# The last 192 columns of a step of experts 0 to 3 take rounded tokens and residuals side by side in one matmul

## The chip, the cores and the metric

The kernel runs on one core of a Trainium2 chip. The metric is the device time of one launch in microseconds: the median of three runs was 637.49 (637.31 to 637.5). A core has a matrix engine (TensorE, PE in the profile, with its weight loads as PEld), VectorE (DVE), ScalarE (ACT), GpSimd (POOL) and SyncE (SP). All run their own instruction streams in order and wait for one another through semaphores. Matmuls read from SBUF and sum into banks of PSUM, which hold 512 float32 values per partition; ACT and DVE take the sums out of there.

## The reference

For 2048 tokens of width 448 the kernel gives `g * a + (1 - g) * b`. Here `a` is the real part of a two-dimensional Fourier transform by dense matrices, `g` a sigmoid of a weighted sum of the token, and `b` a mixture of 8 experts with the two best per token:

```
gates = softmax(xt @ wg);  topk_idx = argsort(-gates)[:, :2];  topk_g normalised to 1
h = gelu(einsum("nd,edf->nef", xt, w1))     # d = 448, f = 1792, tanh form of gelu
y = einsum("nef,efd->ned", h, w2)
b = einsum("ne,ned->nd", cw, y)             # cw: topk_g of the chosen experts, else 0
```

All inputs are float32, and so is the output.

## The kernel before, in words

The transform and the routing come first, up to some 38 us. Then the experts run in the order of their load, each over the tokens that chose it, gathered into columns: `CAPS = (576, 544, 544, 544, 512, 512, 512, 496)` columns for experts 0 to 7. An expert has 14 steps (`NF`), one for each 128 of the 1792 hidden features, so there are 112 jobs `u = (e, f)`.

Both products are made of rounded numbers. A float32 operand is split into a part rounded to the engine's fast type (fp32r) and the residual, rounded too; a product is then hi x hi plus hi x lo plus lo x hi. The tokens of expert `e` stand as `XH[e]` (rounded, 4 chunks of 128 features, the last chunk with its residual in the upper 64 partitions) and `XL[e]` (residuals of the first 3 chunks), written by `turn` (L649 to L660) or, for expert 0, `turn0` and `left0` (L662 to L679). The weights of a job are `hi` and `lo` for the first product, `up` and `dn` for the second, rounded by ACT in `upper` (L205) and by DVE in `lower` (L210).

`up(u)` (L731 to L765) makes the first product and the gelu. Experts 0 to 3 have more than 512 columns and take two halves of `cap // 2`, expert 0 in its first step 256 and 320; experts 4 to 7 take one. Each half is 11 matmuls into one of three `acc` banks: 3 of `hi` with `XH`, 3 of `hi` with `XL`, 1 of `hi` with the last chunk, 4 of `lo` with `XH` (L744 to L747). Before each, its 128x128 weights are loaded. ACT takes the gelu from PSUM into `g` (L748). DVE then casts `g` to `gh` (L756) and subtracts to get `gl` (L757); the columns above 512 are kept apart (L762, or L764 for expert 0).

`down(u)` (L767 to L795) makes the second product: for each of 4 tiles of 128 tokens three matmuls of 448 columns, `gh` with `up`, `gh` with `dn`, `gl` with `up` (L786 to L790), summed over the 14 steps in the banks `Y`. The 32 tokens above 512 of experts 1 to 3 go through `few` (L796 to L811) twice an expert. At an expert's end `combine` (L828) scales the sums, two tiles on DVE and two on ACT, and POOL scatters them into the output.

The order on PE, DVE, ACT and SP is written out by hand. In the main loop (L1034 to L1053) an iteration issues: `turn` of the next expert's tokens if due, rounding of the weights of job `u + 2`, `blocks` (a DVE transpose of gathered tokens, L646) and the gathers on POOL if due, then `up(u + 1)`, `down(u)`, and `side_work`. The last does the checks of the transform's matrices on DVE (two a step for most of experts 1 to 6, L874), the blending of the transform's outputs and their sending. So on DVE the order is weights' residuals, transpose, `gh`, `gl`, rest, checks. On PE a job's second product stands one iteration behind its first.

Of the kernel before, what the change touches and what calls it, by code (L numbers as in the profile page):

```python
# [10 lines left out]
F32R = mybir.dt.float32r  # L11
# [3 lines left out]
AF = mybir.ActivationFunctionType  # L15
OP = mybir.AluOpType
AX = mybir.AxisListType

P = 128
# [4 lines left out]
NC = 4  # L24
# [4 lines left out]
CMAX = max(CAPS)  # L29
# [10 lines left out]
Q = 32  # L40
# [14 lines left out]
LOTS = (0, 6, NF)  # L55
BANKS = (0, 1, 2, 4, 3)
AHEAD = 5
FAR = 65536.0
HERE = 8192.0
SLACK = 2.0 ** -36  # L60
# [2 lines left out]
def r32(ap):  # L63
    return ap.bitcast(F32)


def tiles_of(cap):
    return [min(P, cap - c * P) for c in range((cap + P - 1) // P)]
# [3 lines left out]
def tile_kernel(ctx: ExitStack, tc: tile.TileContext, xt, xrows, xplain, wg, whid, cq, cw, cspec, edge, refs, wquad, whall, cgen, wcat, out):  # L72
    nc = tc.nc
    te, ve, se, gp, sp = nc.tensor, nc.vector, nc.scalar, nc.gpsimd, nc.sync
# [110 lines left out]
    def fetch(k, hold=False):  # L185
        if k >= len(jobs):
            return
        e, f = jobs[k]
        RAW[k] = [stream.tile([P, NC * P], F32, name="raw"), stream.tile([P, D], F32, name="row", bufs=NF - LOTS[1] + AHEAD)]
        if hold:  # L190
# [7 lines left out]
    def apart(e):  # L198
        return CAPS[e] - FULL * P == Q
# [25 lines left out]
    def be(ap):  # L225
        return ap[:, None, :].to_broadcast([P, NT, E])
# [12 lines left out]
    def routing():  # L239
# [89 lines left out]
        ve.tensor_scalar(top, st0, -HERE, None, op0=OP.add)  # L329
        ve.scalar_tensor_tensor(spot, past, FAR, pos, op0=OP.mult, op1=OP.add)  # L330
        ve.tensor_tensor(spot, spot, be(top), OP.add)
# [93 lines left out]
        ve.tensor_tensor(dl, dl, st0, OP.subtract)  # L425
        ve.tensor_scalar(dl, dl, -FAR, None, op0=OP.add)
        ve.tensor_tensor(past, past, be(dl), OP.mult)
# [92 lines left out]


    tl0 = tiles_of(CAPS[0])
    XH, XL = {}, {}

    XG, XQ = {}, {}

# [101 lines left out]
    xp = ctx.enter_context(tc.tile_pool(name="xp", bufs=2))  # L628
# [19 lines left out]

    def turn(e, c):  # L649
        if c == 0:  # L650
            XH[e] = xp.tile([P, NC, CMAX], F32R, name="XH")
            XL[e] = xp.tile([P, NC - 1, CMAX], F32R, name="XL")
        k, xq = XQ.pop((e, c))
        src = xq[:, :k].rearrange("p q c t -> p c q t")
        sl = slice(c * P, c * P + k * Q)
        h = XH[e][:, :, sl].rearrange("p c (q t) -> p c q t", t=Q)
        l = XL[e][:, :, sl].rearrange("p c (q t) -> p c q t", t=Q)
        se.activation(h, src, AF.Copy)
        ve.tensor_tensor(l, src[:, : NC - 1], r32(h[:, : NC - 1]), OP.subtract)
        ve.tensor_tensor(h[64:P, NC - 1], src[64:P, NC - 1], r32(h[64:P, NC - 1]), OP.subtract)  # L660

    def turn0(c, n):  # L662
        if c == 0:
            XH[0] = xp.tile([P, NC, CMAX], F32R, name="XH")
            XL[0] = xp.tile([P, NC - 1, CMAX], F32R, name="XL")
        pt = (psy if c > 1 else ps).tile([P, NC, P], F32, name=f"y{c - 2}" if c > 1 else "acc")
        xg = XG.pop(c)
        for k in range(NC):
            te.transpose(pt[:, k, :n], xg[:n, k * P : (k + 1) * P], ident[:n, :n])  # L669
        sl = slice(c * P, c * P + n)  # L670
        se.activation(XH[0][:, :, sl], pt[:, :, :n], AF.Copy)
        TU[c] = pt, sl, n

    TU = {}

    def left0(c):
        pt, sl, n = TU.pop(c)
        ve.tensor_tensor(XL[0][:, :, sl], pt[:, : NC - 1, :n], r32(XH[0][:, : NC - 1, sl]), OP.subtract)  # L678
        ve.tensor_tensor(XH[0][64:P, NC - 1, sl], pt[64:P, NC - 1, :n], r32(XH[0][64:P, NC - 1, sl]), OP.subtract)  # L679

    def due(e, step, pace):
        c = step // pace
# [2 lines left out]
    def turn_due(e, step, lag, pace):  # L685
        c = due(e, step - lag - 1, pace)
        if c is not None:
            turn(e, c)
# [15 lines left out]
    for m in range(NQT):  # L704
        odd(m, 6)
    turn0(0, tl0[0])
    odd(0, 7)
    left0(0)
    odd(1, 7)
    turn0(1, tl0[1])  # L710
    odd(2, 7)
    left0(1)
    odd(3, 7)
    turn0(2, tl0[2])
    left0(2)
    turn0(3, tl0[3])
    middle()
# [13 lines left out]
    def up(u):  # L731
        e, f = jobs[u]
        hi, lo = W[u]
        cap = CAPS[e]
        rem = max(0, cap - FULL * P)
        g = mp.tile([P, CMAX], F32, name="g")
        nh = 1 if cap <= 512 else 2
        cut = 2 * P if u == 0 else cap // nh
        for hf in range(nh):
            cs = slice(hf * cut, cap if hf == nh - 1 else cut)  # L740
            n = cs.stop - cs.start
            acc = ps.tile([P, 512], F32, name="acc")
            part = lambda w, x, c: (w[:, c * P : (c + 1) * P], x[e][:, c, cs])
            steps = [part(hi, XH, c) for c in range(NC - 1)] + [part(hi, XL, c) for c in range(NC - 1)]  # L744
            steps += [part(hi, XH, NC - 1)] + [part(lo, XH, c) for c in range(NC)]
            for s, (a, b) in enumerate(steps):
                te.matmul(acc[:, :n], a, b, start=s == 0, stop=s == len(steps) - 1)  # L747
            se.activation(g[:, cs], acc[:, :n], AF.Gelu_apprx_tanh)  # L748
        if u == last:
            gh, gl = (stream.tile([P, DX], F32R, name=n) for n in ("hi", "lo"))  # L750
        else:
            gh = mp.tile([P, CMAX + RMAX], F32R, name="gh", bufs=3)
            gl = mp.tile([P, FULL * P], F32R, name="gl", bufs=3)
        main = cap - rem
        top = main if apart(e) else cap
        ve.tensor_copy(gh[:, :top], g[:, :top])  # L756
        ve.tensor_tensor(gl[:, :main], g[:, :main], r32(gh[:, :main]), OP.subtract)  # L757
        if apart(e):
            if f in LOTS:
                rt["rest"] = mp.tile([P, NF - LOTS[1], Q], F32, name="rest", bufs=2)  # L760
            REST[u] = rt["rest"][:, f - max(b for b in LOTS if b <= f)]
            ve.tensor_copy(REST[u], g[:, main:cap])  # L762
        elif rem:
            ve.tensor_tensor(gh[:, cap : cap + rem], g[:, main:cap], r32(gh[:, main:cap]), OP.subtract)  # L764
        GH[u] = (gh, gl)  # L765
# [265 lines left out]

    advance(2)
    up(UP)
    for u in range(UP, last):  # L1034
        e, f = jobs[u]
        plan = (e + 1, f - 1, 2, 2) if e else (1, f - 6, 2, 1)
        turn_due(*plan)
        prep(u + 2)
        if u < UP + SIDE:
            advance(2)  # L1040
            clear(2 * (u - UP))
            clear(2 * (u - UP) + 1)
        if u == last - NF - 1:
            tc.keep_in_program_order(gp.drain())
        if u == UP + SIDE:
            for _ in route:
                pass
            ck = late.enter_context(tc.tile_pool(name="ck", bufs=2, side="right"))
        stage(*plan)
        up(u + 1)  # L1050
        if u < last - 3:
            down(u)
        side_work(u - UP)  # L1053
# [11 lines left out]
    with tc.For_i(0, n_ov) as j:  # L1065
# [25 lines left out]
        pt = ps.tile([P, NC, P], F32, name="acc")  # L1091
# [5 lines left out]
        for f in range(NF):  # L1097
            raw = [stream.tile([P, NC * P], F32, name="raw"), stream.tile([P, D], F32, name="row", bufs=NF - LOTS[1] + AHEAD)]
            for t, b in zip(raw, SIDES):
                sp.dma_start(t, wcat[bass.ds(ej, 1), f, :, b].rearrange("o p n -> (o p) n"))  # L1100
            acc = ps.tile([P, 512], F32, name="acc")
# [18 lines left out]
    with tc.For_i(0, n_a) as j:  # L1120
# [3 lines left out]
        for h in range(2):  # L1124
            hf = full.tile([P, 2 * D], F32, name="hf")
            for u in range(2):
                acc = ps.tile([P, 512], F32, name="acc")
# [4 lines left out]
    with tc.For_i(0, n_b) as i:  # L1132
        acc = psy.tile([P, 512], F32, name="y0")
# [125 lines left out]
```

## Time and profile before

| | us |
|---|---|
| median of three runs | 637.49 |
| the profiled execution | 637.86 |
| its span, first to last instruction | 635.9 |
| PE busy | 625.9 (98%) |
| DVE busy | 506.9 (80%) |
| ACT busy | 248.5 (39%) |
| POOL busy | 205.1 (32%) |

Busy time counts each engine's own instructions in the span of the profiled execution. Matmuls overlap in their pipeline, so a matmul's duration is longer than what it costs; the distance from one start to the next is what it takes of PE's time. A row of the timeline merges neighbours of one kind: the start of the first, the time to the end of the last, and their count behind an x. Behind a row stands the idle time before it in brackets and what ended it.

### The profile page before, as it was taken

Reading aid. Unit: us, or ns where it says so; the run is one execution under the profiler, and the core shown is the slowest. Engines: PE = TensorE matmul, PEld = TensorE weight load, DVE = VectorE, ACT = ScalarE, POOL = GpSimd, SP = SyncE. Lnnn points to the kernel's source line nnn. Section 1 sums busy time; section 2 is a strip of 40 time slices with the busy share of each in tenths; the row PEclk is TensorE's granted clock in tenths of the full one; section 3 lists DMA queues with packets and bytes.
Section 4 is the critical chain, followed back from the end, with each engine's and each line's share of the span. In section 5 each row is a group of like instructions: output and inputs, shape, how many; then the busy total and the mean of one; then the engine's idle time right before and its main releaser. Section 6 shows DMA issues by size and latency. Waiting matters only on the chain.

```text
span 635.9 us, 11090 instructions
## 1 busy us (share of the span) xinstructions
PE 625.9 (98%) x3721; PEld 563.8 (89%) x3721; DVE 506.9 (80%) x1258; ACT 248.5 (39%) x504; POOL 205.1 (32%) x194
## 2 busy tenths in 40 slices
PE   9999999999999999999999999999999999999994
PEld 5999999998998989989899788888888888888884
DVE  7889797689987899779898799988997788555560
ACT  2553233343344434353343534433343434534440
POOL 1210074554144141443340443432331442141123
PEclk9999999999999999999999999999999999999998
DMA  8546454795766865596566767779456737766755
GB/s 346 183 149 210 155 184 140 245 238 192 237 207 160 257 226 197 197 262 196 176 243 234 229 170 244 266 234 276 136 183 195 152 115 150 166 136 145 156 74 65
DMA packets 52319, 122.78 MB, mean 193 GB/s; under 512 B 7488, under 2 KB 32208, under 8 KB 50208
## 3 DMA queue, kind: packets, MB, share of 16 engines
q1 hardware_dynamic: 40944, 101.94, 47.2%
q0 software_dynamic: 11168, 20.00, 18.2%
q8 instruction: 31, 0.51, 0.3%
q14 instruction: 32, 0.26, 0.1%
q10 hardware_dynamic: 144, 0.07, 0.0%
HBM read 105.89 MB, written 16.08 MB: 192 GB/s over the span
## 4 chain that ended last, share of the span: by engine, by line
PE 94%; issue 3%; POOL 1%; DVE 1%; POOLq 0%; ACT 0%; DVEq 0%; ACTq 0%
PE acc L747 45%; PE y L790 42%; PE y L807 1%; PE acc L512 1%; PE y L555 1%; POOL out L843 1%; PE y L474 1%; PE y L116 1%; PE acc L453 0%; POOL out L995 0%; PE acc L404 0%; PE y L669 0%; PE acc L669 0%; POOLq L1028 0%; PE acc L373 0%
## 5 line engine op out<-in xcount | busy, mean ns | idle before, releaser
L748 ACT ACTIVATE g<-acc 128x272 f32<-128x272 f32 (+4 forms) x168 | 78.0, 467 | 318.2 <-issue 178.9
L637 POOL DMA_INDIRECT xg<-xrows,piece x115 | 120.5, 1048 | 226.2 <-DVE xq L646 154.3
L790 PE MATMUL y<-up,gh 128*128 128x448 f32 (+1 forms) x458 | 167.7, 366 | 0.1
L790 PE MATMUL y<-dn,gh 128*128 128x448 f32 (+1 forms) x458 | 167.6, 366 | 0.0
L747 PE MATMUL acc<-XH,hi 128*128 128x272 f32 (+4 forms) x672 | 163.8, 325 | 0.0
L790 PE MATMUL y<-up,gl 128*128 128x448 f32 (+1 forms) x444 | 162.7, 366 | 0.0
L747 PE MATMUL acc<-XH,lo 128*128 128x272 f32 (+4 forms) x672 | 134.9, 322 | 0.0
L747 PEld LDWEIGHTS acc<-XH,hi 128*128 128x128 f32 x672 | 115.2, 188 | 11.2 <-ACT hi L205 1.8
L747 PEld LDWEIGHTS acc<-XH,lo 128*128 128x128 f32 x672 | 105.9, 188 | 8.4
L756 DVE CAST gh<-g 128x512 fp32r<-128x512 f32 (+2 forms) x111 | 48.1, 433 | 81.0 <-ACT g L748 80.6
L747 PE MATMUL acc<-XL,hi 128*128 128x272 f32 (+4 forms) x504 | 107.8, 322 | 0.0
L843 POOL DMA_INDIRECT out<-ys,tok x36 | 61.9, 1721 | 112.5 <-ACT ys L839 71.2
L790 PEld LDWEIGHTS y<-up,gh 128*128 128x128 f32 (+1 forms) x458 | 85.8, 187 | 8.1 <-issue 0.3
L790 PEld LDWEIGHTS y<-dn,gh 128*128 128x128 f32 (+1 forms) x458 | 85.8, 187 | 7.8
L874 DVE CUSTOM_DVE_ANT_0 junk<-quads 128x512 f32<-128x512 f32 x128 | 88.1, 688 | 2.2
L790 PEld LDWEIGHTS y<-up,gl 128*128 128x128 f32 (+1 forms) x444 | 83.2, 187 | 7.3
L747 PEld LDWEIGHTS acc<-XL,hi 128*128 128x128 f32 x504 | 81.0, 188 | 6.9 <-DVE XL L678 0.2
L757 DVE TENSOR_TENSOR gl<-g,gh 128x512 fp32r<-128x512 f32 (+1 forms) x111 | 76.7, 691 | 10.9 <-DVE gh L756 1.4
L210 DVE TENSOR_TENSOR lo<-raw,hi 128x512 fp32r<-128x512 f32 x112 | 77.0, 688 | 1.6 <-ACT hi L205 0.6
L205 ACT ACTIVATE hi<-raw 128x512 fp32r<-128x512 f32 x112 | 69.7, 623 | 0.0
L210 DVE TENSOR_TENSOR dn<-row,up 128x448 fp32r<-128x448 f32 x112 | 69.2, 618 | 0.0
L205 ACT ACTIVATE up<-row 128x448 fp32r<-128x448 f32 x112 | 63.5, 567 | 0.0
(263 smaller groups left out, 389.8 us busy)
## 6 DMA issues: line engine op xcount, KB each, us to landing
quads<-cq SPq DMA_DIRECT2D x16, 2048.0 KB
raw<-wcat SPq DMA_DIRECT2D x112, 256.0 KB
row<-wcat SPq DMA_DIRECT2D x112, 224.0 KB
out<-yt SPq DMA_DIRECT2D x21, 224.0 KB
xraw<-xt SPq DMA_DIRECT2D x8, 512.0 KB
out<-ot POOLq DMA_DIRECT2D x16, 224.0 KB
cw<-cw SPq DMA_DIRECT2D x4, 512.0 KB
xg<-xrows,piece POOLq DMA_INDIRECT x115
```

What stands on the lines that cost most here:

```text
L116: te.matmul(idle, warm[:, :P], warm, start=True, stop=True)
L205: se.activation(hi[:, : raw.shape[-1]], raw, AF.Copy)
L210: ve.tensor_tensor(lo[:, :n], raw, r32(hi[:, :n]), OP.subtract)
L474: te.matmul(LT[c][j : j + 32], wgr[:, cc, far], XR[c][:, r, cc, far, 1 - h if far else h], start=s == 0, stop=s == 3, tile_position=(0, j))
L637: st = gp.indirect_dma_start(out=xg[:, q], out_offset=None, in_=xrows, in_offset=bass.IndirectOffsetOnAxis(ap=rt["piece"][:, e, g : g + 1] ...
L747: te.matmul(acc[:, :n], a, b, start=s == 0, stop=s == len(steps) - 1)
L748: se.activation(g[:, cs], acc[:, :n], AF.Gelu_apprx_tanh)
L756: ve.tensor_copy(gh[:, :top], g[:, :top])
L757: ve.tensor_tensor(gl[:, :main], g[:, :main], r32(gh[:, :main]), OP.subtract)
L790: te.matmul(Y[c][:m, :D], a, b, start=f == 0 and s == 0, stop=f == NF - 1 and s == len(steps) - 1)
L843: st = gp.indirect_dma_start(out=out, out_offset=bass.IndirectOffsetOnAxis(ap=rt["tok"][:n, e, c : c + 1], axis=0), in_=ys[:n], in_offset= ...
L874: ve.tensor_tensor_reduce(out=junk[:, :512], in0=qd[:, a[0], a[1] * 512 : a[1] * 512 + 512], in1=qd[:, b[0], b[1] * 512 : b[1] * 512 + 512 ...
```

## The change

`XH` and `XL` become one tile `X` of 7 chunks: 0 to 3 are the old `XH`, 4 to 6 the old `XL`. The blocks of experts 0 to 3 are no longer halves: the last one has 192 columns (`DUO`), the first the rest, 352 of 544 or 384 of 576. Only the first step of expert 0 stays at 256 and 320. In the last block the three matmuls of `hi` with a chunk of `XH` and the three with its residual become three with 384 columns, chunk and residual side by side; their sums land in two halves of the bank. The five others (192 columns) add to the first half. So the second block has 8 matmuls in place of 11. Then ACT copies the second half into `g`, DVE adds the first half to it, and ACT takes the gelu of `g` in place.

```
-        cut = 2 * P if u == 0 else cap // nh
+        cut = 2 * P if u == 0 else cap - DUO
...
-            part = lambda w, x, c: (w[:, c * P : (c + 1) * P], x[e][:, c, cs])
-            steps = [part(hi, XH, c) for c in range(NC - 1)] + [part(hi, XL, c) for c in range(NC - 1)]
-            steps += [part(hi, XH, NC - 1)] + [part(lo, XH, c) for c in range(NC)]
-            for s, (a, b) in enumerate(steps):
-                te.matmul(acc[:, :n], a, b, start=s == 0, stop=s == len(steps) - 1)
-            se.activation(g[:, cs], acc[:, :n], AF.Gelu_apprx_tanh)
+            part = lambda w, x, c: (w[:, c * P : (c + 1) * P], X[e][:, x + c, cs], n)
+            both = hf == 1 and u > 0
+            if both:
+                steps = [(hi[:, c * P : (c + 1) * P], X[e][:, c : c + NC + 1 : NC, cs], 2 * n) for c in range(NC - 1)]
+            else:
+                steps = [part(hi, 0, c) for c in range(NC - 1)] + [part(hi, NC, c) for c in range(NC - 1)]
+            steps += [part(hi, 0, NC - 1)] + [part(lo, 0, c) for c in range(NC)]
+            for s, (a, b, m) in enumerate(steps):
+                te.matmul(acc[:, :m], a, b, start=s == 0, stop=s == len(steps) - 1)
+            if both:
+                se.activation(g[:, cs], acc[:, n : 2 * n], AF.Copy)
+                ve.tensor_tensor(g[:, cs], acc[:, :n], g[:, cs], OP.add)
+            se.activation(g[:, cs], g[:, cs] if both else acc[:, :n], AF.Gelu_apprx_tanh)
...
-            XH[e] = xp.tile([P, NC, CMAX], F32R, name="XH")
-            XL[e] = xp.tile([P, NC - 1, CMAX], F32R, name="XL")
+            X[e] = xp.tile([P, 2 * NC - 1, CMAX], F32R, name="X")
...
-        h = XH[e][:, :, sl].rearrange("p c (q t) -> p c q t", t=Q)
-        l = XL[e][:, :, sl].rearrange("p c (q t) -> p c q t", t=Q)
+        h = X[e][:, :NC, sl].rearrange("p c (q t) -> p c q t", t=Q)
+        l = X[e][:, NC:, sl].rearrange("p c (q t) -> p c q t", t=Q)
```

`turn0` and `left0` are changed in the same way as `turn`.

## Rows read from the trace of the kernel before

**Rows 1.** The page's chain of work that ended last, as shares of the span: by engine, then by engine, tile and line.

```profile
PE 94%; issue 3%; POOL 1%; DVE 1%; POOLq 0%; ACT 0%; DVEq 0%; ACTq 0%
PE acc L747 45%; PE y L790 42%; PE y L807 1%; PE acc L512 1%; PE y L555 1%; POOL out L843 1%; PE y L474 1%; PE y L116 1%; PE acc L453 0%; POOL out L995 0%; PE acc L404 0%; PE y L669 0%; PE acc L669 0%; POOLq L1028 0%; PE acc L373 0%
```

**Rows 2.** Busy time of each engine in the stretches of experts 0 to 3 (from the second step of expert 0 on). Columns: stretch and its length, then busy time and count of PE, PEld, DVE, ACT, POOL, the granted clock as a share of full speed, DMA share, GB/s.

```profile
41.14:124.66 83.52, 83.52 (x570) 79.80 (x569) 67.15 (x170) 27.35 (x60) 27.89 (x25) 1.00 0.57 185
124.66:201.49 76.83, 76.78 (x510) 70.92 (x508) 66.42 (x165) 32.18 (x71) 27.90 (x23) 1.00 0.68 216
201.49:278.14 76.65, 76.65 (x512) 70.99 (x509) 67.04 (x171) 31.49 (x69) 25.17 (x22) 1.00 0.71 225
278.14:347.82 69.68, 69.68 (x462) 65.74 (x459) 60.11 (x152) 27.89 (x61) 23.47 (x20) 1.00 0.69 216
```

**Rows 3.** Timeline of PE in expert 1: the first matmuls of one step's first product, the first of the second product behind it, and the first of the second product one step later. Columns: start and length in us, engine, line, operation, tiles, shape, count.

```profile
135.42 0.54 PE L747 MATMUL acc<-XH,hi 128*128 128x272 f32 x3
...
138.19 0.36 PE L790 MATMUL y<-up,gh 128*128 128x448 f32 x1
...
143.43 0.36 PE L790 MATMUL y<-up,gh 128*128 128x448 f32 x1
```

**Rows 4.** Timeline of PE: rows of the first product at 256, 320 and 512 columns, each with the start of the row that follows it.

```profile
38.87 0.64 PE L747 MATMUL acc<-XH,lo 128*128 128x256 f32 x4
39.34 0.60 PE L747 MATMUL acc<-XH,hi 128*128 128x320 f32 x3
...
40.55 0.75 PE L747 MATMUL acc<-XH,lo 128*128 128x320 f32 x4
41.14 0.56 PE L747 MATMUL acc<-XH,hi 128*128 128x288 f32 x3
...
404.76 0.84 PE L747 MATMUL acc<-XL,hi 128*128 128x512 f32 x3
405.44 0.39 PE L747 MATMUL acc<-XH,hi 128*128 128x512 f32 x1
```

**Rows 5.** Timeline of PE before the experts: unrounded matmuls of 113 columns (two passes each, both counted) and transposes of 128, each with the start of the row that follows it.

```profile
9.97 2.04 PE L512 MATMUL acc<-wr,fr 128*128 128x113 f32 x16
11.94 1.19 PE L474 MATMUL y<-xraw,wgr 128*32 128x128 f32 x32
...
36.06 0.60 PE L669 MATMUL y<-ident,up 128*128 128x128 f32 x4
36.49 0.60 PE L669 MATMUL y<-ident,dn 128*128 128x128 f32 x4
```

**Rows 6.** Timeline of ACT and DVE, a step of expert 1 in which DVE waits, and a transpose of expert 0 with the activation that waits for it; then three groups of the instructions by line and shape (count, busy us, mean ns of one, idle us before).

```profile
138.38 0.40 ACT L748 ACTIVATE g<-acc 128x272 f32<-128x272 f32 x1 [0.94 <-PE acc L747]
138.82 0.43 DVE L756 CAST gh<-g 128x512 fp32r<-128x512 f32 x1 [1.48 <-ACT g L748]
139.35 0.69 DVE L757 TENSOR_TENSOR gl<-g,gh 128x512 fp32r<-128x512 f32 x1
139.96 0.17 DVE L762 COPY rest<-g 128x32 f32<-128x32 f32 x1
...
112.43 0.71 DVE L646 STREAM_TRANSPOSE xq<-xg 128x512 f32<-128x512 f32 x1
113.17 0.63 ACT L658 ACTIVATE XH<-xq 128x512 fp32r<-128x512 f32 x1 [2.10 <-DVE xq L646]
...
L678 DVE TENSOR_TENSOR XL<-y,XH 128x192 fp32r<-128x192 f32 x1 | 0.4, 358 | 0.0
L748 ACT ACTIVATE g<-acc 128x512 f32<-128x512 f32 x42 | 25.2, 600 | 110.9 <-issue 83.4 <-PE acc L747 23.6 <-ACT up L205 3.9
L837 DVE TENSOR_SCALAR ys<-y,wgt 128x448 f32<-128x448 f32 x16 | 10.3, 677 | 4.7 <-PE y L790 4.7
```

**Rows 7.** What DVE waited for (us in total, times, longest us), in the stretches 41.14 to 126 us (two rows, expert 0 and the first cast of expert 1), 126 to 201.5 (expert 1, that first cast included), 201.5 to 278.1 (expert 2), 278.1 to 347.8 (expert 3) and 347.8 to 430 (expert 4 and a step more), in this order.

```profile
DVE gh L756 <- ACT g L748: 10.4, 6, 5.7
DVE wgt L407 <- PE acc L747: 3.5, 1, 3.5
...
DVE gh L756 <- ACT g L748: 12.3, 8, 5.7
...
DVE gh L756 <- ACT g L748: 7.0, 6, 2.3
...
DVE gh L756 <- ACT g L748: 7.0, 7, 2.1
...
DVE gh L756 <- ACT g L748: 6.1, 6, 1.9
```

**Rows 8.** Timeline of PE and DVE in expert 2: the start of the second product behind the first of a step, and the cast of that step's `g`, for two steps.

```profile
214.84 0.36 PE L790 MATMUL y<-up,gh 128*128 128x448 f32 x1
...
216.70 0.62 DVE L756 CAST gh<-g 128x512 fp32r<-128x512 f32 x1
...
225.32 0.36 PE L790 MATMUL y<-up,gh 128*128 128x448 f32 x1
...
227.94 0.42 DVE L756 CAST gh<-g 128x512 fp32r<-128x512 f32 x1
```

**Rows 9.** Timeline of PE and DVE at the first step of expert 0: its first matmuls, and a write of DVE into another part of the same tile.

```profile
37.93 0.62 PE L747 MATMUL acc<-XH,hi 128*128 128x256 f32 x3
...
38.25 0.29 DVE L679 TENSOR_TENSOR XH<-y,XH 64x128 fp32r<-64x128 f32 x1
```

More of the change, by code (lines that the diff above doesn't have):

```diff
@@ L57 @@
 AHEAD = 5
+DUO = 192
 FAR = 65536.0
@@ L522, in tile_kernel @@
     tl0 = tiles_of(CAPS[0])
-    XH, XL = {}, {}
+    X = {}
     XG, XQ = {}, {}
@@ L663, in turn0 @@
         if c == 0:
-            XH[0] = xp.tile([P, NC, CMAX], F32R, name="XH")
-            XL[0] = xp.tile([P, NC - 1, CMAX], F32R, name="XL")
+            X[0] = xp.tile([P, 2 * NC - 1, CMAX], F32R, name="X")
         pt = (psy if c > 1 else ps).tile([P, NC, P], F32, name=f"y{c - 2}" if c > 1 else "acc")
@@ L670, in turn0 @@
         sl = slice(c * P, c * P + n)
-        se.activation(XH[0][:, :, sl], pt[:, :, :n], AF.Copy)
+        se.activation(X[0][:, :NC, sl], pt[:, :, :n], AF.Copy)
         TU[c] = pt, sl, n
@@ L677, in left0 @@
         pt, sl, n = TU.pop(c)
-        ve.tensor_tensor(XL[0][:, :, sl], pt[:, : NC - 1, :n], r32(XH[0][:, : NC - 1, sl]), OP.subtract)
-        ve.tensor_tensor(XH[0][64:P, NC - 1, sl], pt[64:P, NC - 1, :n], r32(XH[0][64:P, NC - 1, sl]), OP.subtract)
+        ve.tensor_tensor(X[0][:, NC:, sl], pt[:, : NC - 1, :n], r32(X[0][:, : NC - 1, sl]), OP.subtract)
+        ve.tensor_tensor(X[0][64:P, NC - 1, sl], pt[64:P, NC - 1, :n], r32(X[0][64:P, NC - 1, sl]), OP.subtract)
     def due(e, step, pace):
```

## The prediction

> **What bounds the kernel now.** I read the chain of waits first: 94% of it is TensorE (PE), 45% in the experts' first product (L747) and 42% in the second (L790) [rows 1]. The reader is to see that hardly anything else stands in that chain. Then the stretches of experts 0 to 3: PE is busy for all of each, at the full clock, VectorE (DVE) 80 to 87% and ScalarE (ACT) 33 to 42% [rows 2]. So a step costs what PE's instructions cost, and DVE has the least room behind it. Then one step of expert 1 on PE: 22 matmuls of 272 columns take 2.77 us (135.42 to 138.19), and the same place comes round 5.24 us later (143.43) [rows 3]. The matmul durations overlap, so I take the distance between starts (the pitch) as their cost.
>
> **Step 1, the pitch on PE.** The pitch is 0.118 us at 256 columns, 0.126 at 272, 0.1475 at 320 and 0.227 at 512 [rows 3, 4]: some 0.42 ns a column and some 13 ns of its own per matmul. The columns don't change: before, a 544-token step streams 22 x 272 = 5984; after, 11 x 352 + 3 x 384 + 5 x 192 = 5984. Only three matmuls fall away, 3 x 13 = 39 ns at most.
>
> The doubtful term is a matmul of 192 columns with its own 128x128 weights. No such row exists. Along the slope it would be 0.126 - 80 x 0.00042 = 0.092 us. But no matmuls with full weights of four bytes stand that close in these rows: the transposes of 128 columns are 0.1075 us apart (36.06 to 36.49, four), and L512, 113 columns in two passes each, 0.123 us (9.97 to 11.94, sixteen) [rows 5]. Both stream fewer columns than 256, and their pitch doesn't shrink in proportion. I take 0.115, midway between these two, with 0.092 and 0.123 as ends.
>
> The Trainium skill (TensorE: Matmul & The Clock Gate, section on LDWEIGHTS) has a weight load last its columns over 1.2 GHz, an estimate of 107 ns for 128 columns, which is longer than 192 columns stream; its section on the weight-path modes denies FP32 the fast load. By it these matmuls pay for their weights and not for their columns, which speaks against narrow ones. The transposes' 0.1075 agrees, L512 lies above; with 0.107 the sum below would be +9.0 us and the median 646.5.
>
> So a step of experts 1 to 3 is 11 x 0.161 + 3 x 0.174 + 5 x 0.115 = 2.87 us against 2.77, +0.10 (ends: -0.02 and +0.14). In expert 0, 13 steps (its first stays as it was): 11 x 0.174 + 3 x 0.174 + 5 x 0.115 = 3.01 against 22 x 0.1325 = 2.92 along the slope, also +0.10. Over 13 + 42 = 55 steps PE alone is +5.4 us (ends -0.9 and +7.6). Whatever the pitch, PE gains next to nothing.
>
> **Step 2, the added pair on DVE and ACT.** After the second block PE's sum lies in two halves. ACT copies one, DVE adds the other, ACT takes the gelu, and only then can DVE cast `gh`. ACT's copy runs where its gelu ran, and ACT has room. On DVE two things are new. The add: 192 elements from PSUM took 0.358 us [rows 6]. And a hole, since add and cast are neighbours in DVE's order with a gelu between them: DVE to ACT 0.03 us (transpose done at 113.14, ACT starts at 113.17), the gelu of 192 elements by the slope from 272 (0.40) to 512 (0.60) 0.33, ACT to DVE 0.04 (ACT done at 138.78, cast at 138.82) [rows 6]. Together 0.76 us of DVE's time per step. The ends: 0.42, if the add cost what the copy of 32 elements does (0.17) less the 0.08 by which neighbours overlap (`gl` at 139.35 lasts 0.69, the next starts 0.61 later), and the gelu were the whole hole; and 1.0, if the two handovers and the add's own wait for ACT's copy each cost 0.1, as the pause between cast and `gl` does (139.25 to 139.35) [rows 6].
>
> Has DVE that room? It waits for `g` 12.3 us in expert 1, 5.7 of them at once at its start, so 6.6 inside; 7.0 in expert 2; 7.0 in expert 3 [rows 7]. The pair needs 14 x 0.76 = 10.6 us an expert, and PE's own 14 x 0.10 = 1.4 us gives DVE that much more. Left over: 10.6 - 6.6 - 1.4 = 2.6, then 2.2 and 2.2, together 7.0 us. For steps on end DVE has no wait left already: its casts at 216.70 and 227.94 follow the ends of the first products (214.84 and 225.32) by 1.9 and 2.6 us, where on time is 0.63 (138.19 to 138.82) [rows 3, 6, 8].
>
> A late DVE does no harm until `gl` is late for PE. On time, `gl` is done at 140.04, and the second product that reads it begins at 143.43 [rows 3, 6]: 3.4 us, less 0.76, plus 0.4 since only its third matmul reads `gl`, so 3.0 us may be owed. Expert 4, with 6.1 us of waits [rows 7], pays them back. So 7.0 - 3.0 = 4.0 us land on PE, as holes ahead of the second product.
>
> In expert 0, 13 x 0.76 = 9.9 us stand against 1.3 us from PE, waits of 10.4 - 5.7 = 4.7 for `g` and one of 3.5 at L407 [rows 7]; 0.4 is left, which may be owed into the 5.7. Nothing; 0.9 us if the wait at L407 is of no use.
>
> **Step 3, what is queued behind.** Behind ACT's gelu, which now waits for a late DVE, stand the roundings of the weights after next. DVE subtracts from them after cast, `gl` and rest, when ACT has had over a microsecond. The weights' DMAs issue after that subtract, three steps ahead, and the gathers on POOL wait for DVE's transpose and are used two steps later: up to 3 us of lateness cost them nothing.
>
> **Step 4, one tile in place of two.** The first step's matmuls started at 37.93 while DVE still wrote other columns of the same tile from 38.25 on [rows 9]: waits go by region, and merging costs nothing.
>
> **Sum.** 5.4 + 4.0 = +9.4 us on the profiled 637.86 (span 635.9 and 1.96 around it) is 647.3; the median of 637.49 lies 0.37 lower, so 646.9. It hardly hangs on the pitch: at 0.092 PE gives -0.9 and DVE's debt is 4.2 + 3.8 + 3.8 - 3.0 = 8.8, so +7.9 (645.4); at 0.123, 7.6 + 2.3 = +9.9 (647.4). It hangs on the pair: at 0.42 the debt is gone, +5.4 (642.9); at 1.0 it is 6.0 + 5.6 + 5.6 - 3.0 = 14.2, +19.6 (657.1).
>
> **Rivals.**
> *DVE has room and narrow matmuls are cheap* (the other side). Three matmuls fewer at 13 ns on 55 steps give -2.2 us, 635.3. It needs a pitch near 0.092 and a pair below 7.0 / 14 = 0.50 us; from there on PE sets every step. For it: PE is busy throughout, and nothing in the chain waits for `gl` now [rows 1, 2]. Against: rows 5 and step 2.
> *DVE has room, PE pays for its weights.* The debt never reaches PE: +5.4 at 0.115, +1 near 0.097; 638.5 to 643, say 641. For it: waits come and go, and where DVE would wait anyway part of the pair may be swallowed. Against: the casts without a wait [rows 8].
> *Narrow matmuls stream slower than a column a cycle.* The rows show this type at 256 columns and more. At two cycles, pitch 0.173: 55 x 0.39 = +21 us with DVE hidden behind it, 659; at four, 0.333: 55 x 1.19 = +65, 703. For it: only that no row excludes it. Against: the slope is the same from 256 to 512 [rows 4].
> *A late DVE also holds the combining at the ends of experts.* The scaled sums stand behind `gl` and rest on DVE (0.17 and 0.68 [rows 6]), and the next expert's first matmul writes the same bank: with the 0.4 some 1.2 us less may be owed at three ends, +3.6, and a pair of 0.85 adds 42 x 0.09 = 4: 650.5 to 654.5.
>
> **How the numbers follow.** The forecast has 0.55, with its own range of 642 to 650; the faster rival 0.12, PE alone 0.13, slower streaming 0.12, the ends of experts 0.08. The range that leaves out slow streaming and half of the faster rival is 635.5 to 655. About 0.2% (1.3 us) is what a measurement here can tell from no change: faster by more 0.12; within it 0.08, the edges of the faster rival and of PE alone; slower 0.80.
>
> **What would show it.** Step 1: 192-column matmuls 0.107 to 0.123 us apart. Step 2: waits of 0.4 us between add and cast in every step, casts 0.7 us or more later after the first product, and holes of PE ahead of the second product in experts 1 to 3 that end with DVE's `gl`, 4 us together. No such holes in a longer time would be PE alone; a first product of 3.1 us or more, slower streaming; one of 2.75 us and no holes, the faster rival.

## The result, and the profile after

The changed kernel takes 642.42 us in the median of six runs (642.26 to 642.76), beside it the kernel before 637.5: a ratio of 1.008, interval 1.0069 to 1.0091, or 4.9 us more. Forecast were 9.4 more, 646.9, in a range of 635.5 to 655. The direction and the two places were right, the size was twice too large.

The page's lines of the changed kernel, as in the table of before:

```profile
span 640.4 us, 10875 instructions
PE 630.7 (98%) x3556; PEld 567.8 (89%) x3556; DVE 523.3 (82%) x1313; ACT 261.9 (41%) x559; POOL 206.9 (32%) x194
```

165 matmuls fewer, three in each of 55 steps, and PE is busy 4.8 us longer. In the numbering of the changed kernel the first product is L750, the second L796, the copy L752, the add L753, the gelu L754, the cast L762, `gl` L763, the weights' residuals L211.

One step of expert 1 on PE, timeline (answers to [rows 3, 4]); columns are start, length, engine, line, operation, tiles, shape, count:

```profile
141.65 1.28 PE L750 MATMUL acc<-X,hi 128*128 128x352 f32 x7
...
142.77 0.80 PE L750 MATMUL acc<-X,lo 128*128 128x352 f32 x4
...
143.41 0.78 PE L750 MATMUL acc<-X,hi 128*128 128x384 f32 x4
...
144.03 0.61 PE L750 MATMUL acc<-X,lo 128*128 128x192 f32 x4
...
144.48 0.39 PE L796 MATMUL y<-up,gh 128*128 128x448 f32 x1
```

The four last matmuls of 192 columns stand (144.48 - 144.03) / 4 = 0.1125 us apart. The row before merges the three of 384 with the first of 192. A short window (144.11 to 144.15) shows that first one by itself:

```profile
143.94 0.25 PE L750 MATMUL acc<-X,hi 128*128 128x192 f32 x1
144.03 0.39 PE L750 MATMUL acc<-X,lo 128*128 128x192 f32 x2
```

So a wide one takes (143.94 - 143.41) / 3 = 0.177 us, and the first narrow one, right behind a wide one, only 0.09. The first product takes 2.83 us (2.77 before), and a step 144.48 - 139.19 = 5.29 us, the second product of the step before having begun at 139.19; it was 5.24.

The same step on DVE and ACT, timeline (answers to [rows 6]); in brackets the idle time before and what ended it:

```profile
139.38 0.33 ACT L752 ACTIVATE g<-acc 128x192 f32<-128x192 f32 x1 [0.54 <-PE acc L750]
...
139.75 0.36 DVE L753 TENSOR_TENSOR g<-acc,g 128x192 f32<-128x192 f32 x1 [0.18 <-ACT g L752]
...
140.14 0.36 ACT L754 ACTIVATE g<-g 128x192 f32<-128x192 f32 x1 [0.42 <-DVE g L753]
...
140.54 0.43 DVE L762 CAST gh<-g 128x512 fp32r<-128x512 f32 x1 [0.43 <-ACT g L754]
...
141.00 0.69 DVE L763 TENSOR_TENSOR gl<-g,gh 128x512 fp32r<-128x512 f32 x1
```

Copy, add, gelu, cast follow one another as the forecast had it: from the add to the cast 0.79 us (140.54 - 139.75), 0.43 of it a hole. What DVE waited for in expert 2 (204 to 281 us; answers to [rows 7]; us in total, times, longest):

```profile
DVE gh L762 <- ACT g L754: 5.2, 12, 0.4
DVE gh L762 <- issue: 0.9, 2, 0.4
DVE g L753 <- ACT g L752: 0.2, 1, 0.2
```

Before, DVE had 7.0 us of waits there in six pieces of up to 2.3. Now there are fourteen of 0.4, the holes, and next to nothing ahead of the add: DVE is early at hardly any step. Where that reaches PE is seen in the timeline of expert 2 (PE, and DVE's `gl`):

```profile
233.22 0.39 PE L796 MATMUL y<-up,gh 128*128 128x448 f32 x1
233.44 0.37 PE L796 MATMUL y<-dn,gh 128*128 128x448 f32 x1
233.79 0.47 PE L796 MATMUL y<-up,gl 128*128 128x448 f32 x1
...
233.04 0.69 DVE L763 TENSOR_TENSOR gl<-g,gh 128x512 fp32r<-128x512 f32 x1
```

The third matmul, the first to read `gl`, starts 0.35 us after the second in place of 0.2: `gl` was done at 233.73. And over 126 to 352 us what PE's weight loads waited for:

```profile
PEld y L796 <- DVE gl L763: 1.4, 4, 0.4
...
PEld acc L750 <- DVE lo L211: 0.7, 2, 0.4
```

### The profile page after: what moved, and what is told of

The parts are those of the page before. It is cut to its first block, busy times and chain, and to the rows that moved or that the text cites. A ratio compares the mean times of both kernels' runs of the same rounds, so it can differ in the third digit from the quotient of the medians.

```text
span 640.4 us, 10875 instructions
## 1 busy us (share of the span) xinstructions
PE 630.7 (98%) x3556; PEld 567.8 (89%) x3556; DVE 523.3 (82%) x1313; ACT 261.9 (41%) x559; POOL 206.9 (32%) x194
## 5 line engine op out<-in xcount | busy, mean ns | idle before, releaser
L750 PE MATMUL acc<-X,hi 128*128 128x352 f32 (+5 forms) x1011 | 216.3, 349 | 0.0
L638 POOL DMA_INDIRECT xg<-xrows,piece x115 | 122.0, 1061 | 240.0 <-DVE g L753 96.1
L750 PEld LDWEIGHTS acc<-X,hi 128*128 128x128 f32 x1011 | 179.1, 188 | 17.9 <-ACT hi L206 0.7
L796 PE MATMUL y<-up,gh 128*128 128x448 f32 (+1 forms) x458 | 168.5, 368 | 0.1
L796 PE MATMUL y<-dn,gh 128*128 128x448 f32 (+1 forms) x458 | 167.5, 366 | 0.0
L796 PE MATMUL y<-up,gl 128*128 128x448 f32 (+1 forms) x444 | 162.7, 367 | 0.0
L750 PE MATMUL acc<-X,lo 128*128 128x192 f32 (+5 forms) x672 | 139.7, 330 | 0.1
L754 ACT ACTIVATE g<-acc 128x352 f32<-128x352 f32 (+4 forms) x113 | 59.4, 526 | 178.4 <-issue 94.0
L750 PEld LDWEIGHTS acc<-X,lo 128*128 128x128 f32 x672 | 109.1, 189 | 9.2 <-DVE lo L211 0.7
L762 DVE CAST gh<-g 128x512 fp32r<-128x512 f32 (+2 forms) x111 | 48.3, 435 | 71.3 <-ACT g L754 66.3
L796 PEld LDWEIGHTS y<-up,gh 128*128 128x128 f32 (+1 forms) x458 | 86.1, 188 | 7.7 <-DVE ys L843 0.3
L796 PEld LDWEIGHTS y<-dn,gh 128*128 128x128 f32 (+1 forms) x458 | 86.1, 188 | 7.3
L796 PEld LDWEIGHTS y<-up,gl 128*128 128x128 f32 (+1 forms) x444 | 83.3, 188 | 8.5 <-DVE gl L763 1.4
L763 DVE TENSOR_TENSOR gl<-g,gh 128x512 fp32r<-128x512 f32 (+1 forms) x111 | 76.8, 692 | 7.2
L211 DVE TENSOR_TENSOR lo<-raw,hi 128x512 fp32r<-128x512 f32 x112 | 77.0, 687 | 1.6 <-ACT hi L206 0.6
L754 ACT ACTIVATE g<-g 128x192 f32<-128x192 f32 x55 | 20.1, 365 | 127.4 <-DVE g L753 113.5
L211 DVE TENSOR_TENSOR dn<-row,up 128x448 fp32r<-128x448 f32 x112 | 69.2, 618 | 0.0
L1001 POOL DMA_DIRECT2D out<-ot x16 | 13.8, 865 | 60.3 <-ACT ot L1000 60.3
```

The source lines that it names most:

```text
L211: ve.tensor_tensor(lo[:, :n], raw, r32(hi[:, :n]), OP.subtract)
L638: st = gp.indirect_dma_start(out=xg[:, q], out_offset=None, in_=xrows, in_offset=bass.IndirectOffsetOnAxis(ap=rt["piece"][:, e, g : g + 1] ...
L750: te.matmul(acc[:, :m], a, b, start=s == 0, stop=s == len(steps) - 1)
L754: se.activation(g[:, cs], g[:, cs] if both else acc[:, :n], AF.Gelu_apprx_tanh)
L796: te.matmul(Y[c][:m, :D], a, b, start=f == 0 and s == 0, stop=f == NF - 1 and s == len(steps) - 1)
L1001: st = gp.dma_start(out[i * P : (i + 1) * P, :], ot[:, :D], accum_op=OP.add)
```

## The experiments

The theory: the 4.9 us are two parts, PE's own pitch and holes of PE that a late DVE leaves. Rival A has the pitch alone, rival B the late DVE alone. Each run is compared with runs of the kernel before on the same chip, 637.17 us for the first four and 637.35 for the others.

**e1_no_pair.** The pair is taken out.

```
-            if both:
-                se.activation(g[:, cs], acc[:, n : 2 * n], AF.Copy)
-                ve.tensor_tensor(g[:, cs], acc[:, :n], g[:, cs], OP.add)
-            se.activation(g[:, cs], g[:, cs] if both else acc[:, :n], AF.Gelu_apprx_tanh)
+            se.activation(g[:, cs], acc[:, :n], AF.Gelu_apprx_tanh)
```

> The changed kernel without the pair: the second block keeps its 8 matmuls, but ACT takes the gelu straight from the first half of the bank; ACT's copy and DVE's add are gone, so the residuals' product of the last 192 columns is left out in experts 0 to 3. Theory (two parts: about 3.1 us are PE's own pitch, 55 steps x 0.05 to 0.06 us, and about 2 us are holes of PE that a late DVE leaves): 640.6 us, no PE wait for DVE in experts 1 to 3, the first product still 2.83 us a step. Rival A (PE's pitch is all of it, the holes would have come anyway): 642.4. Rival B (the late DVE is all of it): 637.5 with a first product of 2.77 us.

Measured: 640.05 us, ratio 1.0045 (1.0031 to 1.0059), +2.9. PE waits for DVE nowhere between 126 and 352 us, and the step is 5.29 us as in the changed kernel. So PE's matmuls cost 2.9 us by themselves, and neither rival holds. DVE's waits in expert 2 are again like those before the change:

```profile
DVE gh L759 <- ACT g L751: 7.2, 8, 1.7
```

**e2_pair_alone.** The matmuls of before, with the pair on the last 192 columns.

```
+            if hf == 1 and u > 0:
+                ds = slice(cap - DUO, cap)
+                se.activation(g[:, cs.start : ds.start], acc[:, : n - DUO], AF.Gelu_apprx_tanh)
+                se.activation(g[:, ds], acc[:, n - DUO : n], AF.Copy, scale=0.0)
+                ve.tensor_tensor(g[:, ds], acc[:, n - DUO : n], g[:, ds], OP.add)
+                se.activation(g[:, ds], g[:, ds], AF.Gelu_apprx_tanh)
...
```

> The kernel before with the pair alone: 11 matmuls of half the columns as before, but for the last 192 columns ACT first copies the sum times zero into g, DVE adds the sum, then ACT takes the gelu (the other columns of that half get their gelu first). Same values. Theory: PE's matmuls as before (2.77 us), DVE needs some 0.65 us a step more, 9.0 us an expert against waits of 6.6, 7.0 and 7.0, and since PE isn't slowed it gets no more room: holes of 4 us, 641.5 us. Rival A (PE's pitch is all): 637.5. Rival B (late DVE is all): 642.4.

Measured: 641.13 us, ratio 1.0063 (1.0049 to 1.0077), +4.0. Its first product starts 5.25 us after the one before (135.78 and 141.03), as fast as before, and PE's weight loads wait for DVE (126 to 352 us):

```profile
PEld acc L748 <- DVE lo L211: 2.4, 4, 0.8
PEld y L798 <- DVE gl L765: 1.8, 9, 0.2
```

These are 4.2 us, against 2.1 in the changed kernel. The two parts alone, 2.9 and 4.0, are more than the whole of 4.9. That fits a slower PE that leaves DVE more time, so that each part hides some of the other; the sum is rough, since ACT has one instruction more a step in e2 than in the changed kernel.

**e3_dn_between.** The changed kernel with one DVE instruction moved into the hole: `lower` makes only `lo` at its old place, and `flush` makes the `dn` that it put off (in steps without the pair, ahead of the first block).

```
                 ve.tensor_tensor(g[:, cs], acc[:, :n], g[:, cs], OP.add)
+                flush()
...
```

> The changed kernel with one DVE instruction moved: the subtract that makes dn (0.62 us, the residuals of the second product's weights two steps on) is issued between the add and the cast in place of ahead of the add, so that ACT's gelu runs under it. Same values, same work. Theory (the hole between add and cast is what makes DVE late): DVE's need falls to the add alone, 14 x 0.34 = 4.8 us an expert, less than the old waits; PE's holes go, 640.6 us. Rival C (the add's own time or the copy's wait makes DVE late): 642.4. Rival A: 642.4.

Measured: 640.06 us, ratio 1.0047 (1.0033 to 1.0061), the time of e1. DVE's timeline around the add (L765), with `dn` (L218) and the cast (L775) behind it:

```profile
173.21 0.35 DVE L765 TENSOR_TENSOR g<-acc,g 128x192 f32<-128x192 f32 x1
173.48 0.61 DVE L218 TENSOR_TENSOR dn<-row,up 128x448 fp32r<-128x448 f32 x1
174.01 0.42 DVE L775 CAST gh<-g 128x512 fp32r<-128x512 f32 x1
```

The cast starts without a wait, the add is still there, and PE has no wait for DVE between 126 and 352 us. The hole between add and cast is what made DVE late; the add alone fits into the room it had.

**e4_256_no_pair.** As e1, with `DUO = 256`.

> As e1_no_pair, with the last 256 columns in place of 192 (blocks of 288 and 256, in expert 0 320 and 256; side by side 512 columns); the residuals' product of these 256 columns is left out. Theory (a matmul of 192 columns takes 0.115 us because of its weights, one of 256 is paid by its columns): 11 x 0.1325 + 3 x 0.218 + 5 x 0.118 = 2.70 us a step in place of 2.77, expert 0 2.87 for 2.92: 42 x 0.07 + 13 x 0.05 = 3.6 us less than before, 633.9. Rival (narrow matmuls pay by their columns and it is the side by side form that costs): like e1, 640.6.

Measured: 634.5 us, ratio 0.9962 (0.9948 to 0.9975), 2.7 faster than before. The step on PE:

```profile
139.75 1.09 PE L750 MATMUL acc<-X,hi 128*128 128x288 f32 x7
140.68 0.69 PE L750 MATMUL acc<-X,lo 128*128 128x288 f32 x4
141.21 0.97 PE L750 MATMUL acc<-X,hi 128*128 128x512 f32 x4
142.01 0.63 PE L750 MATMUL acc<-X,lo 128*128 128x256 f32 x4
142.48 0.37 PE L793 MATMUL y<-up,gh 128*128 128x448 f32 x1
```

The first product takes 2.73 us, with 256 columns 0.1175 apart. Side by side costs nothing of its own: three of 512 and one of 256 in 0.80 us are 0.2275 for a wide one, as in [rows 4]. A matmul of 192 columns costs 0.1125, one of 256 0.1175: the 64 columns between them are nearly free, which is why 192 lost.

**e7_128_no_pair** and **e8_cut_alone** measure that further: e1 with `DUO = 128`, and the kernel before with

```
-        cut = 2 * P if u == 0 else cap // nh
+        cut = 2 * P if u == 0 else cap - DUO
```

(`DUO = 192`) and nothing else.

> As e1_no_pair with the last 128 columns (blocks of 416 and 128, in expert 0 448 and 128; side by side 256 columns); leaves the residuals' product of these columns out. It measures the pitch of matmuls of 128 columns. Theory (below 256 columns a matmul pays for its weights): pitch 0.107 to 0.115 as at 192, step 11 x 0.188 + 3 x 0.118 + 5 x 0.11 = 2.97 against 2.77, together 648 us. Rival (pay by the column, with a larger constant part): pitch 0.065 to 0.09, step 2.75 to 2.87, 636 to 643.

> The kernel before with blocks of 352 and 192 (expert 0 384 and 192) and 11 matmuls in each, no side by side, no pair. Same values. Theory: 11 x 0.160 + 11 x 0.115 = 3.02 us a step against 2.77, 55 x 0.25 = 14 us slower, 651 us; what the side by side form then gives back is 651 - 640 = 11 us. Rival (narrow columns cost nothing, the side by side form costs): 637.5.

Measured: 646.64 us (ratio 1.0147, 1.0131 to 1.0162) and 648.02 us (1.0168, 1.0153 to 1.0184). The rows of e7 on PE, then those of e8:

```profile
140.82 0.61 PE L750 MATMUL acc<-X,lo 128*128 128x128 f32 x4
141.27 0.41 PE L793 MATMUL y<-up,gh 128*128 128x448 f32 x1
```

```profile
139.97 0.48 PE L748 MATMUL acc<-XH,hi 128*128 128x192 f32 x3
...
141.18 0.39 PE L791 MATMUL y<-up,gh 128*128 128x448 f32 x1
```

128 columns: 0.1125 us. Eleven matmuls of 192 in e8: (141.18 - 139.97) / 11 = 0.110. So from 128 to 192 columns the pitch stays where it is, and both rivals of a price by the column fall. The first narrow matmul of a block is the exception: behind a wide one it takes 0.09 us at 192 columns (above) and 0.06 at 128, as this step of e7 shows:

```profile
146.16 0.22 PE L750 MATMUL acc<-X,hi 128*128 128x128 f32 x1
146.22 0.39 PE L750 MATMUL acc<-X,lo 128*128 128x128 f32 x2
```

So it isn't the columns that take 0.11 us. The weight loads of the changed kernel (PEld, the step shown first) start (143.94 - 143.25) / 4 = 0.17 us apart at the wide matmuls and (144.38 - 143.94) / 4 = 0.11 apart at the narrow ones:

```profile
143.25 0.70 PEld L750 LDWEIGHTS acc<-X,hi 128*128 128x128 f32 x4
143.94 0.52 PEld L750 LDWEIGHTS acc<-X,lo 128*128 128x128 f32 x4
144.38 0.19 PEld L796 LDWEIGHTS y<-up,gh 128*128 128x128 f32 x1
```

The narrow matmuls keep step with the loads. That the loads set the pace is read from these distances; no run changed the loads alone. The expectation of e8 was 3 us too high, since I had put 0.115. Between e8 and e1, 10.7 and 2.9 us above before, lies what the side by side form does give back on the same blocks: 7.8 us. The change took it, after having paid more for the narrow block.

The Trainium skill (TensorE: Matmul & The Clock Gate, section on LDWEIGHTS) has a load take its columns over 1.2 GHz, an estimate of 107 ns for 128 columns. The 0.110 to 0.1125 us here agree with it within 6 ns. The middle of my two rows, 0.115, was a little high.

**e5_256_between.** e4's columns and e3's order together, nothing left out.

> The changed kernel with 256 columns in the last block and DVE's dn subtract moved between add and cast (e3_dn_between and e4_256_no_pair together). Nothing is left out. Theory: PE saves as in e4 (2.7 us less than before), and with the hole filled DVE's need is the add, some 14 x 0.4 = 5.6 us an expert against waits of 6.6 to 7.0: 634.5 to 635 against 637.2, faster than both kernels. Rival (a quicker PE takes back the room of DVE): holes return, 637 or more.

Measured: 635.52 us, ratio 0.9969 (0.9956 to 0.9981): faster than both kernels, 1.8 us below before. It lies a little above the expectation. Against e4 some 0.4 us stand in two first products, of experts 2 and 3, that take 2.93 and 2.95 us in place of 2.72 (from 226.18 and 302.34); there PE waits for DVE's `lo`. The rest was not followed up.

**e6_256_pair.** The changed kernel with `DUO = 256` and nothing else.

> The changed kernel with 256 columns in place of 192 and nothing else. Theory (DVE's debt): the pair grows to an add of 0.41 and a hole of 0.48, PE's step is 0.05 us shorter than before, so about 10.6 us an expert are needed against waits of 6.6, 7.0 and 7.0 and less time to do it in: holes of 8 to 11 us, 643 to 646 us, slower than the changed kernel although its matmuls are quicker. Rival A (PE's pitch decides): 634.5 to 636.

Measured: 651.47 us, ratio 1.0221 (1.0207 to 1.0235), slower than any other, with quicker matmuls than the changed kernel. The theory gave the sign and fell short by 5 us or more. PE's waits for DVE (42 to 362 us):

```profile
PEld y L796 <- DVE gl L763: 6.8, 18, 0.5
PEld acc L750 <- DVE lo L211: 4.8, 7, 1.6
...
PEld y L796 <- DVE gh L762: 2.0, 3, 1.5
...
PEld y L796 <- DVE rest L768: 1.2, 1, 1.2
```

Two things were missing in my sum. Expert 0 pays too: from its first matmul to expert 1's it is 83.78 us (37.72 to 121.50) against 80.64 in e4 (37.93 to 118.57). And nothing is owed from one expert to the next. In the fourth step of expert 1 DVE has caught up (the cast at 144.12 follows the first product's end, 142.45, by 1.67 us), and each expert pays for itself: expert 2 takes 81.14 (201.23 to 282.37) for 75.96 (193.13 to 269.09). Without anything owed, the need of 3 x 10.6 less waits of 20.6 is 11.2, PE's shorter steps make it 42 x 0.05 = 2.1 more, and expert 0 adds 3.1: 16.4 us. From the first matmul of expert 0 to that of expert 4, e6 takes 17.2 more than e4 (37.72 to 362.03 against 37.93 to 345.05). e5 differs from e6 in the place of one subtract, and in 16 us.

## Why the prediction was half right

*Step 1, the pitch.* The price of a narrow matmul behind another was right, 0.115 put and 0.1125 measured, that of a wide one nearly so, 0.174 put and 0.177 in the step shown, and the columns that stay constant gained nothing. Mis-sized was the first narrow one, for which I had put 0.115 like the others: it takes 0.09. The block of 352 took 0.01 less than forecast, and the four other narrow ones together another 0.01. So a step is 2.83 us and not 2.87, and the second product behind it 0.01 shorter: +0.05 a step, and 2.9 us (e1) in place of 5.4.

*Step 2, the pair on DVE.* Its make-up was right: the add and a hole that waits for ACT's gelu, 0.79 us put together for 0.76 forecast, and e3 shows the hole alone to be decisive. The debt was too large: about 2 us of holes (642.42 against e1) where 4.0 were forecast, although PE gave DVE less time than I had thought. The traces show where the holes lie. From an expert's first matmul to the next expert's, experts 0 to 3 of the changed kernel take 81.93, 76.77, 78.32 and 77.99 us (starts at 37.76, 119.69, 196.46, 274.78 and 352.77), those of e1 81.91, 75.95, 77.38 and 77.39 (37.67, 119.58, 195.53, 272.91 and 350.30). That is nothing in expert 0, as forecast, and 0.82, 0.94 and 0.60 us in the others, together 2.4. Two terms of the sum failed.

The first is what is left over in an expert, 10.6 - 7.0 - 1.4 = 2.2 us in expert 2 by forecast. Here are 14 of its steps, from the cast of its third to the cast of expert 3's third, in the kernel before and in the changed one (columns as in [rows 2]):

```profile
210.23:286.88 76.65, 76.65 (x510) 70.99 (x509) 66.18 (x166) 31.49 (x69) 25.15 (x22) 1.00 0.72 217
213.07:291.39 78.32, 78.25 (x468) 71.98 (x467) 70.17 (x181) 34.47 (x83) 27.01 (x22) 1.00 0.67 213
```

DVE is busy 4.0 us longer, and 14 holes of 0.43 are 6.0, so the pair costs 10.0. DVE was idle for 10.5 us and is now for 8.2, which without the holes is 2.1: the pair found room of 8.3 us, where I had counted 7.0 of waits. PE's own pitch gave 0.7 and not 1.4. Left over is 10.0 - 8.3 - 0.7 = 1.0 us, the 0.94 of holes.

Part of the room that I had missed lay ahead of `gl`. In the kernel before, 0.10 us stood between cast and `gl`, and I took it for the price of a handover [rows 6]. An instruction of its own that waits stands there. The rows of the line of `gl` (first the kernel before, then the changed one; DVEq is DVE's sequencer; times are min/median/max in ns, then the first and last start):

```profile
L757 DVEq EVENT_SEMAPHORE  x87: 21/21/21, 139.3 to 619.3; - x87
```

```profile
L763 DVEq EVENT_SEMAPHORE  x49: 21/21/21, 368.4 to 624.2; - x49
```

In experts 1 to 3 it is gone: the pause between cast and `gl` is 0.03 us now (140.97 to 141.00). That gives 0.07 us back in 37 of the 42 steps, some 0.9 us an expert. It is the pair that takes it away: the count is 87 in every kernel without it (before, e1, e4, e7, e8) and 49 in every one with it (the changed one, e2, e3, e5, e6). That `gl` has two semaphores to wait for, and that the add, which has waited for PE already, makes the second one needless, is argued and not shown.

The second is the 3.0 us that may be owed until expert 4 pays them back. Their size was about right: on time, the cast now stands 1.35 us behind the end of the first product, and the first hole ahead of `gl` in expert 1 comes where it is 4.6 behind (172.40 and 177.03), 3.3 later. But nothing is carried to expert 4. In the third step of expert 2, DVE is on time again:

```profile
211.72 0.39 PE L796 MATMUL y<-up,gh 128*128 128x448 f32 x1
...
213.07 0.43 DVE L762 CAST gh<-g 128x512 fp32r<-128x512 f32 x1 [0.43 <-ACT g L754]
```

It is so in the third step of expert 3 too (290.04 and 291.39). At the change of experts a step of PE takes 7.0 us in place of 5.3 (196.46 to 203.49), and there DVE catches up. The holes stand in a few steps in the midst of an expert, where the lateness is largest: the step from 230.05 to 237.28 takes 7.23 us, for 6.65 in e1 (229.11 to 235.76). So each expert pays its own rest, and a credit of 3.0 for all three is not there. With it, the rests of about 1 us an expert would have left no holes at all: the two errors partly cancel in the forecast of 4.0.

*Step 3, what is queued behind.* Among PE's waits from 126 to 352 us there is none for a DMA or a gather, as forecast. But `lo` does come late for PE at times (0.7 us in the changed kernel, 4.8 in e6), since it stands behind a late `gl` on DVE. I had held only `gl` to be dangerous.

*Step 4, one tile.* The first product starts at 37.76 us (37.93 before), and e4 with the merged tile is the faster kernel: no cost to be seen.

*The rivals.* "DVE has room, PE pays for its weights" is e1, not the changed kernel. The time alone would not have told: 642.42 lies within that rival's 638.5 to 643 and only just within the forecast's own 642 to 650. The waits, e1 and e3 decide. The faster rival needed a pitch of 0.092, and slower streaming more than 0.17; the rows exclude both. Of holding at expert ends there is one wait of PE's loads for DVE's `ys` (L843), 0.3 us.

## What to carry to other kernels

Where every matmul loads its own 128x128 weights of four bytes, narrow matmuls in a row went at the pace of the loads: 128, 192 and 256 columns cost 0.1125, 0.1125 and 0.1175 us here, so merge such blocks until they are at least 256 wide. A small pair of operations on two engines in strict order costs the engine not its busy time but the round trip; put work that isn't urgent between the two (16 us between e6 and e5 for the place of one subtract). And read an engine's room as the sum of its waits by stretch, not as one minus its busy share; then see in the trace when it is on time again, for until there lateness adds up and no further.

## What was not expected of the hardware

In these traces DVE's `gl` is led by a wait instruction of its own in the kernels without the pair: 0.105 us from cast to `gl` with it (139.24 to 139.35 in the kernel before), 0.035 without. A narrow matmul behind a wide one takes 0.06 us at 128 columns and 0.09 at 192, but 0.11 behind another narrow one. The pitch of 128 columns is not below that of 192, and three matmuls fewer in a step made no less time until the narrow ones were widened. A quicker PE made the kernel slower: e6, with a first product some 0.1 us a step shorter than the changed kernel's, is 9 us behind it.
